# Local and global attention with a gated layer behind it: first loads through another queue, strips by copies, weights in eight loads

## The chip, the core and the metric

The kernel runs on one core of a Trainium2 chip. The time is the device time of one execution in microseconds; less is better. The core has five engines with queues of their own: TensorE (PE), VectorE (DVE), ScalarE (ACT), GpSimd (POOL) and SyncE (SP). PEld in the profile is TensorE's weight load. Transfers are issued here by SyncE and by GpSimd, and both queues share 16 DMA engines. A transfer that changes the type of the data (float32 to float16) is issued by GpSimd in this kernel; SyncE's keep the type.

## What is computed

```
# q_l, k_l, v_l: (8 batches, 8 heads, 512, 64); q_g, k_g, v_g: (8, 8, 32, 64); float32
k_all, v_all = concat(k_g, k_l), concat(v_g, v_l)
out_g = softmax(q_g k_all^T / 8) v_all                      # 32 global rows see everything
s_ll  = where(|i - j| <= 32, q_l k_l^T / 8, -1e9)           # 512 local rows: a band of 65 keys
out_l = softmax(concat(q_l k_g^T / 8, s_ll)) v_all          # and the 32 global keys
x = concat(out_g, out_l), heads side by side                # (8 * 544, 512)
h = x @ w_in                                                # (4352, 2048)
out = (h * clip(h + 3, 0, 6) / 6) @ w_out                   # (4352, 512)
```

## The kernel before

**Layout and stages.** Matmul operands are float16. A batch has four tiles of 128 local rows (`j`), and each tile four units of 32 rows (`u`). For each tile the steps are:

- load: `load_qk` (two transfers of 128 x 8 x 64 values, q into `nat[:, 0]` and k into `nat[:, 1]`), `load_v` into `ve`, `load_g` into `natg`;
- turn: `turn_qk` transposes eight 128 x 128 blocks on TensorE (L471) into the one PSUM tile `t` and copies them to `qk`; `turn_g` does the same for the global rows (L487, `gt`);
- scores: `local_step` writes into PSUM `s`. Where `kept` is true (`b < KEPT`) each unit's 96 keys stand in the order in which the strip holds them, cut in pieces, with 32-row matmuls for the global keys (L527, 80 matmuls a tile); otherwise 8 matmuls (L534) and 32 (L541);
- softmax, for each of eight heads: VectorE adds the mask, takes the minimum of the negated scores and writes `sm` (L553); ScalarE takes exponentials (L564); VectorE scales four heads at a time into `pn` (L578); TensorE transposes (L585); a copy takes `et` out of `t`;
- values: `av` multiplies `et` with strips `st`: for each unit, the 96 rows of v that it may see and the 32 global rows (L603 in batches 0 and 1, L608 later). The result goes from PSUM `a` to `xt`.

`global_steps` does the 32 global rows of a batch. The strips are made from `ve` in one of two ways: `strips_kept`, copies on ScalarE or VectorE, or `strips_moved`, seven transfers by SyncE's queue (L435).

The gated layer follows: `first` multiplies with `win` (L713), ScalarE computes `t` (L720), VectorE the product `gs` (L724); `second` multiplies `gs` with `wout` (L735), a copy takes `ot` out and SyncE stores it (L750). Batch 0 goes through `first` in parts of 128 rows, batch 1 of 256, the others of 512 (`PART`).

**Order.** Nothing is scheduled on the chip. Each step is added to a `Plan` with the engines that can do it, a duration for each (ns), its predecessors, a key (lower is more urgent) and the rings of buffers that it takes and frees. `Plan.lay` goes through time and writes the order of each engine's instructions; a step that two engines can do (`BOTH`) goes to one of them by a rule. `Transfers` stands in for the DMA queues, eight in flight on each. `Plan.fill` puts matmuls on a tile of zeros (`idle`, L850) into gaps of TensorE that the plan shows before the first step of the gated layer. On the chip each engine runs its list in that order and waits where a predecessor isn't done: a constant changed in the plan moves instructions everywhere.

**Beginning.** GpSimd's queue starts with q and k of tile 0, then the selects that make `ident` and the mask's band, then k_g, tile 1 and the rest by `seq` (`v` a part of v, `i` a quarter of w_in, `g` the other global rows). VectorE clears tiles (`clear`) and makes six masks (`mask_steps`): 3 to 5 for the kept order, 0 to 2 for the other. w_in comes in 16 transfers of 128 x 512 values (`load_w_in`), w_out in 16 (`load_w_out`), w_out behind batch 1's loads by its keys.

Of the kernel before, what the change touches and what calls it, by code (L numbers as in the profile page):

```python
# [26 lines left out]
class Transfers:  # L27
# [4 lines left out]
    FIRST, SHARE = {"POOL": 2400, "SP": 2700}, {"POOL": 0.65, "SP": 0.35}  # L32
# [41 lines left out]
class Plan:  # L74
# [4 lines left out]
    COLD, FILL = 5150.0, 216.0  # L79
# [17 lines left out]
    def lay(self):  # L97
        free = {e: 1240 if e == "POOL" else 0 for e in self.LAT}
# [27 lines left out]
        while len(order) < len(self.ops):  # L126
            best = None
            behind = {e: sum(o.can[e] for o in cand if len(o.can) == 1 and not o.dma) for e, cand in opened.items()}
            for e, cand in opened.items():
# [5 lines left out]
                for o in cand:  # L135
                    s = max(free[e], ready[o])
                    if len(o.can) > 1 and any(max(free[k], ready[o]) + d + behind[k] < s + o.can[e] + behind[e]
                                              for k, d in o.can.items() if k != e):
                        continue
                    if o.acq:  # L140
                        s = max(s, min(rings[o.acq]))
                    if o.dma:
                        t = move.lane_free(o, e)
                        s = INF if t is None else max(s, t)
                    if s < INF:
                        starts.append((s, o))
# [3 lines left out]
                s, o = min(((s, o) for s, o in starts if s <= s0 + 40), key=lambda x: (x[1].key, x[1].n))  # L150
                if best is None or s < best[0]:
                    best = (s, o, e)
# [20 lines left out]
            else:  # L173
                o.fin = s + dur + self.LAT[o.eng]
# [4 lines left out]
    def fill(self, order, emit):  # L179

        at, out = 900.0, []
        for o in order:
            if o.eng == "PE" and at is not None:
                one = self.FILL * (2 if at < self.COLD else 1)
                for _ in range(int((o.start - at - 150) / one)):
                    out.append(Op("PE", one, emit, (), 0, None, (), 0, None))
                at = None if o.acq == "M" else max(at, o.start + o.dur)
# [5 lines left out]
def kernel(  # L193
# [83 lines left out]
    def copy(op, out, in_):  # L277
        if op.eng == "ACT":
            nc.scalar.copy(out=out, in_=in_)  # L279
        else:  # L280
            nc.vector.tensor_copy(out=out, in_=in_)  # L281

    BOTH = ("ACT", "DVE")
    SCALE = ("DVE", 600)
# [10 lines left out]
    def mask_steps():  # L295
# [5 lines left out]
        z = add("DVE", 250, a, key=-9)  # L301
# [7 lines left out]
        z = add("POOL", 700, b, [z], key=-7.98)  # L309
# [7 lines left out]
        z = add("DVE", 700, c, [z], key=-9)  # L317

        def d():
            nc.vector.tensor_copy(out=masks[5], in_=m)  # L320
            nc.vector.memset(masks[5][P - UQ:P, UQ:2 * UQ], OUTSIDE)
            for u in range(NU):
                nc.vector.tensor_copy(out=w[u * UQ:(u + 1) * UQ, G:P], in_=m[0:UQ, 0:KL])
            nc.vector.tensor_copy(out=masks[0], in_=w)
            nc.vector.memset(masks[0][0:UQ, G:G + UQ], OUTSIDE)
            nc.vector.tensor_copy(out=masks[2], in_=w)
            nc.vector.memset(masks[2][P - UQ:P, P - UQ:P], OUTSIDE)
        prep["masks"] = add("DVE", 1000, d, [z], key=-3.5)
        return z

    def ident_step():
# [7 lines left out]
        return add("POOL", 400, b, [z], key=-7.99)  # L339

    def clear():
        for r in range(2):
# [3 lines left out]
            nc.vector.memset(kgz[r], 0.0)  # L346
            nc.vector.memset(pg[r][:, S:], 0.0)
            nc.vector.memset(ve[r][:, NJ, :], 0.0)
        nc.vector.memset(natg[0], 0.0)

    prep["ident"] = ident_step()
    prep["clear"] = add("DVE", 2000, clear, key=-10)
# [8 lines left out]
    ROW, WIDE, LONG, STORE, SHORT = 13.6, 80.0, 175.0, 92.0, 72.0  # L361
# [23 lines left out]

    def load_v(b, i, key):
# [12 lines left out]
    TIGHT, AHEAD, KEPT, PART = 2, 6.0, 1, {0: 128, 1: 256}  # L399

    def strips_kept(b, js, key):
# [8 lines left out]
        def put(dst, src, deps):  # L410
            o.append(add(BOTH, (160 + 730 * n, 60 + 140 * n), lambda op: copy(op, dst, src), deps + before,
# [41 lines left out]
    def load_w_in(g, key):  # L453
        return [load(lambda op, m=m: w_in_t[:, m, g * 512:(g + 1) * 512],
                     moe_w_in[m * P:(m + 1) * P, g * 512:(g + 1) * 512], P, key + 0.001 * m, ns=WIDE)
                for m in range(NP)]

    def load_w_out(c, key):
        return load(lambda op: w_out_t[:, c, :], moe_w_out[c * P:(c + 1) * P, :], P, key, ns=WIDE)
# [3 lines left out]
    def turn_qk(b, j, ld, key):  # L463
        r = b % 2

        def pe(op):
            ps = psT[op.slot]
            for i in range(2):
                for p in range(NP):
                    c0 = (i * NP + p) * P  # L470
                    nc.tensor.matmul(out=ps[:, c0:c0 + P], lhsT=nat[ld[0].slot][:, i, p * P:(p + 1) * P],  # L471
                                     rhs=ident, is_transpose=True)
        t = add("PE", 450, pe, [*ld, prep["ident"]], key=key, acq="T", rel=ld[:1])

        def ev(op):
            copy(op, qk[r][:, :, :, UQ + j * P:UQ + (j + 1) * P],
                 psT[t.slot].rearrange("d (i p s) -> d p i s", i=2, p=NP))
# [3 lines left out]
        return add(BOTH, (900, 600), ev, deps, key=key, rel=[t])  # L481
# [28 lines left out]
    def local_step(b, j, key):  # L510
# [3 lines left out]
        m_op = prep["mask"] if kept and j < NJ - 1 else prep["masks"]  # L514
# [29 lines left out]
        s = add("PE", 900 if kept else 600, pe, [qkT[b, j], qkT[b, min(j + 1, NJ - 1)], kg[b]], key=key, acq="S")  # L544
# [4 lines left out]
        for h in range(H):  # L549
# [10 lines left out]
            t = add("DVE", 212, red, [s, sm_op, m_op], key=key + 0.01 * h, rel=[s])  # L560
# [70 lines left out]
    def global_steps(b, key):  # L631
# [5 lines left out]
        for e in range(2):  # L637
# [10 lines left out]
            s = add("PE", 360, pe, [gT[b // 2]] + [qkT[b, j] for j in range(NJ)], key=key + 0.2 * e, acq="S")  # L648
# [81 lines left out]
    def second(t0, gdone, set_, dests, keys):  # L730
        f = None
        for q in range(4):
# [4 lines left out]
            deps = gdone[q * 4:q * 4 + 4] + [wo[c] for c in range(q * 4, q * 4 + 4)]  # L737
# [50 lines left out]
    lqk, lg = {}, {}  # L788
# [98 lines left out]
```

## Time and profile before

| | before |
|---|---|
| median of 3 runs | 366.24 us (363.99 to 366.33) |
| profiled execution: time, span | 366.75 us, 365.0 us |
| granted clock of TensorE, mean | 0.984 |
| TensorE busy | 342.1 us (94%), 4407 matmuls |
| VectorE, ScalarE, GpSimd busy | 286.1, 249.9, 120.9 us |
| moved by DMA | 41.89 MB: 17.57 by GpSimd's queue, 23.60 by SyncE's |
| matmuls on the idle tile | 51, 14.4 us |

The span is the time from the first to the last instruction. Matmuls are pipelined and their ends are modelled, so a busy TensorE may also be one that waits. In lines of the profile, `out<-in` names tiles without buffer numbers, shapes are partitions x elements, `L` numbers are lines of the kernel, and the part in brackets is the idle time of the engine before the instruction and what ended it. Copies of the helper `copy` all have line L281 on VectorE and L279 on ScalarE, and every load by GpSimd has L365.

### The profile page before, as it was taken

The numbers are of one execution on the slowest core, as the hardware profiler recorded it, in microseconds if no ns is written. First come the engines' busy times: TensorE is split into PE (matmuls) and PEld (weight loads), VectorE is DVE, ScalarE is ACT, GpSimd is POOL, SyncE is SP. The second block draws the span as 40 slices with busy tenths as digits, with TensorE's granted clock in tenths as the row PEclk, the third lists the DMA queues.
The fourth block names the chain that finished last, engine by engine and source line by source line (L and its number), as shares of the span: only waits on it lengthen the run. The fifth ranks groups of instructions, "written<-read, shape, count | busy, mean of one in ns | idle before, by whom it ended". The sixth has DMA issues, their size and how long they took to land.

```text
span 365.0 us, 11304 instructions
## 1 busy us (share of the span) xinstructions
PE 342.1 (94%) x4407; PEld 204.1 (56%) x4407; DVE 286.1 (78%) x1018; ACT 249.9 (68%) x772; POOL 120.9 (33%) x167
## 2 busy tenths in 40 slices
PE   6985986999899999999999999999999999999995
PEld 2555883556885665456555654555455444445642
DVE  7799888679898999788898989889988996166300
ACT  0686885679895799687976797558974885165411
POOL 8978855870293603135421531060000000000000
PEclk9999897899999999999999999999999999999999
DMA  9999999999699999539991999099001100110012
GB/s 65 138 175 135 171 224 206 99 190 247 86 139 225 138 179 203 39 75 166 234 68 59 141 225 105 31 132 246 32 2 59 61 2 0 59 57 0 31 48 97
DMA packets 123205, 41.89 MB, mean 115 GB/s; under 512 B 108432, under 2 KB 116112, under 8 KB 123152
## 3 DMA queue, kind: packets, MB, share of 16 engines
q0 software_dynamic: 111104, 17.57, 65.6%
q1 hardware_dynamic: 12048, 23.60, 22.8%
q8 instruction: 34, 0.56, 0.6%
q14 instruction: 19, 0.16, 0.2%
HBM read 35.13 MB, written 8.91 MB: 121 GB/s over the span
## 4 chain that ended last, share of the span: by engine, by line
PE 60%; DVE 19%; DMA 6%; ACT 6%; POOL 4%; issue 3%; SPq 0%; POOLq 0%; ACTq 0%; DVEq 0%
PE m L735 28%; PE m L713 20%; DVE gs L724 5%; DVE sm L553 4%; DMA win<-in_moe_w_in_dram 3%; DVE pn L578 3%; PE t L585 3%; DVE xt L281 2%; ACT sm L564 2%; PE a L608 2%; POOL nat L365 2%; ACT t L720 2%; PE t L471 2%; DMA st<-ve 2%; PE s L541 1%
## 5 line engine op out<-in xcount | busy, mean ns | idle before, releaser
L735 PE MATMUL m<-wout,gs 128*128 128x512 f16 x544 | 131.7, 385 | 0.6 <-DVE gs L724 0.6
L713 PE MATMUL m<-xt,win 128*128 128x512 f16 (+2 forms) x768 | 124.9, 310 | 5.5 <-DVE gs L724 3.2
L564 ACT ACTIVATE sm<-sm,stat 128x128 f32<-128x128 f32 x256 | 99.8, 393 | 20.1 <-DVE stat L553 19.9
L724 DVE SCALAR_TENSOR_TENSOR gs<-t,m 128x512 f16<-128x512 f32 x136 | 90.7, 682 | 23.4 <-ACT t L720 22.7
L713 PEld LDWEIGHTS <-win 128*128 128x128 f16 x832 | 69.2, 99 | 51.8 <-issue 8.2
L720 ACT ACTIVATE t<-m 128x512 f32<-128x512 f32 x136 | 80.0, 595 | 23.9 <-PE m L713 21.2
L735 PEld LDWEIGHTS <-gs 128*128 128x128 f16 x544 | 50.4, 99 | 51.7 <-issue 2.9
L553 DVE CUSTOM_DVE_ANT_0 sm<-s,mask 128x128 f32<-128x128 f32 x256 | 60.0, 284 | 8.4 <-PE s L541 7.9
L365 POOL DMA_DIRECT2D nat<-in_q_l_dram x32 | 28.7, 898 | 102.0 <-PE t L471 95.3
L564 ACT ACTIVATION_READ_ACCUMULATOR sm<-sm,stat 128x1 f32 x256 | 48.7, 190 | 0.0
L578 DVE TENSOR_TENSOR pn<-sm,stat 128x512 f16<-128x512 f32 x64 | 44.0, 688 | 1.1
L365 POOL DMA_DIRECT2D ve<-in_v_l_dram x40 | 32.4, 835 | 0.1
L279 ACT CAST xt<-a 64x512 f16<-64x512 f32 (+1 forms) x36 | 20.8, 577 | 15.7 <-PE a L608 12.5
L279 ACT COPY ot<-m 128x512 f32<-128x512 f32 x21 | 12.2, 582 | 25.9 <-PE m L735 23.0
L365 POOL DMA_DIRECT2D nat<-in_k_l_dram x32 | 29.2, 911 | 0.1
L585 PE MATMUL t<-ident,pn 128*128 128x128 f16 x256 | 20.3, 222 | 3.5 <-issue 1.7
L585 PEld LDWEIGHTS <-pn 128*128 128x128 f16 x256 | 17.0, 99 | 9.6 <-issue 4.5
L471 PE MATMUL t<-ident,nat 128*128 128x128 f16 x256 | 19.9, 219 | 1.6 <-DMA nat<-in_k_l_dram 1.4
L553 DVE DVE_READ_ACCUMULATOR2_ANT stat<- 128x1 f32 x256 | 21.0, 82 | 0.0
L471 PEld LDWEIGHTS <-nat 128*128 128x128 f16 x256 | 16.3, 98 | 7.5 <-DMA nat<-in_k_l_dram 1.7
L281 DVE COPY et<-t 128x1024 f16<-128x1024 f16 x22 | 15.1, 687 | 6.7 <-PE t L585 5.7
L281 DVE CAST xt<-a 64x512 f16<-64x512 f32 (+1 forms) x20 | 13.8, 690 | 5.4 <-ACT xt L279 4.4
(76 smaller groups left out, 322.1 us busy)
## 6 DMA issues: line engine op xcount, KB each, us to landing
out_dram<-ot SPq DMA_DIRECT2D x32, 256.0 KB, 3.1
st<-ve SPq DMA_DIRECT2D x14, 384.0 KB, 6.4
nat<-in_q_l_dram POOLq DMA_DIRECT2D x32, 128.0 KB, 4.9
nat<-in_k_l_dram POOLq DMA_DIRECT2D x32, 128.0 KB, 5.1
st<-ve SPq DMA_DIRECT2D x7, 512.0 KB, 6.8
st<-ve SPq DMA_DIRECT2D x14, 256.0 KB, 6.1
ve<-in_v_l_dram POOLq DMA_DIRECT2D x24, 128.0 KB, 4.9
win<-in_moe_w_in_dram POOLq DMA_DIRECT2D x16, 128.0 KB, 5.3
```

The lines of the kernel that those rows point to most:

```text
L279: nc.scalar.copy(out=out, in_=in_)
L281: nc.vector.tensor_copy(out=out, in_=in_)
L365: nc.gpsimd.dma_start(out=dst(op), in_=src)
L471: nc.tensor.matmul(out=ps[:, c0:c0 + P], lhsT=nat[ld[0].slot][:, i, p * P:(p + 1) * P], rhs=ident, is_transpose=True)
L553: nc.vector.tensor_tensor_reduce(out=sm[sm_op.slot][:, h, :], in0=psS[s.slot][:, e, p * P:(p + 1) * P], in1=m, scale=-scale, scalar=3.0e38 ...
L564: nc.scalar.activation(out=sm[sm_op.slot][:, h, :], in_=sm[sm_op.slot][:, h, :], func=EXP, scale=-1.0, bias=stat[stat_op.slot][:, 0, h:h + 1],
L578: (nc.gpsimd if op.eng == "POOL" else nc.vector).tensor_tensor(out=pn[pn_op.slot][:, h0:h1, :], in0=sm[sm_op.slot][:, h0:h1, :], in1=stat[ ...
L585: nc.tensor.matmul(out=psT[op.slot][:, h * P:(h + 1) * P], lhsT=pn[pn_op.slot][:, h, :], rhs=ident, is_transpose=True)
L713: nc.tensor.matmul(out=psM[op.slot][:, i * n:(i + 1) * n], lhsT=w_in_t[:, m, (c + i) * P:(c + i + 1) * P], rhs=x()[:, m, t0:t0 + n], start ...
L720: nc.scalar.activation(out=t1[to.slot], in_=psM[f.slot], func=RELU, bias=0.5, scale=1.0 / 6.0)
L724: nc.vector.scalar_tensor_tensor(out=gs[set_.slot][:, c:c + k, t0:t0 + n], in0=t1[to.slot].rearrange("f (k t) -> f k t", k=k), scalar=1.0, ...
L735: nc.tensor.matmul(out=psM[(f or op).slot], lhsT=gs[set_.slot][:, c, t0:t0 + P], rhs=w_out_t[:, c, :], start=(c == 0), stop=(c == NDFF - 1))
```

## The change

1. **q and k of tiles 0 and 1 of batch 0** are loaded by SyncE's queue as float32 into `sm` (free at that time), and VectorE or ScalarE casts them into `nat` (`load_qk_direct`). `turn_qk` can turn q or k alone: of tile 1, k is loaded and turned ahead of q, and the scores of tile 0 wait for the k parts of both tiles (`keyT`) and their own q part.
2. **Strips of batch 1** are copied too (`KEPT` from 1 to 2, so that batch 1's scores take the kept form), in blocks of one, one and two tiles instead of two and two. GpSimd may do these copies as well (`COPY`).
3. **Masks and clears.** Only masks 3 and 4 are made at the start; the others follow behind the first scores, in pieces that ScalarE or VectorE does (`later`). Some clears become ScalarE copies from `idle`. The selects stand ahead of GpSimd's first load.
4. **Weights** come in four transfers for w_in and four for w_out, 512 rows of 512 values each.
5. **Filled gaps.** The filling goes on until tile 0 of batch 2 is multiplied with its strips, for gaps over 400 ns, and the idle matmuls write `a` instead of `m`.
6. **The plan** has other durations and shares for DMA, and a step that two or three engines can do goes to the one that would end it first, counting only more urgent work ahead of it.

By the order of the instructions, GpSimd has 17 of the strip copies (5 for batch 0, 12 for batch 1). In the whole kernel VectorE has 10 more copies into `et`, 6 more into `eg`, 4 more into `ot` and 7 more of 64 rows into `xt`, and 7 fewer of 1024 columns into `qk`. TensorE has 56 idle matmuls.

```diff
@@ class Transfers, class Plan
-    FIRST, SHARE = {"POOL": 2400, "SP": 2700}, {"POOL": 0.65, "SP": 0.35}
+    FIRST, SHARE = {"POOL": 2400, "SP": 2400}, {"POOL": 0.55, "SP": 0.45}
-    COLD, FILL = 5150.0, 216.0
+    COLD, FILL = 5000.0, 216.0
+    AHEAD, WAIT = 0.3, 0.0
@@ lay
-                    if len(o.can) > 1 and any(max(free[k], ready[o]) + d + behind[k] < s + o.can[e] + behind[e]
-                                              for k, d in o.can.items() if k != e):
-                        continue
+                    if len(o.can) > 1:
+                        ends = {k: max(free[k], ready[o]) + d + sum(
+                            x.can[k] for x in opened[k] if len(x.can) == 1 and not x.dma and x.key < o.key
+                            and ready[x] < max(free[k], ready[o]) + 100) for k, d in o.can.items()}
+                        if min(ends.values()) < ends[e]:
+                            continue
@@ fill
-                for _ in range(int((o.start - at - 150) / one)):
-                    out.append(Op("PE", one, emit, (), 0, None, (), 0, None))
-                at = None if o.acq == "M" else max(at, o.start + o.dur)
+                if o.start - at > 400:
+                    out += [Op("PE", one, emit, (), 0, None, (), 0, None) for _ in range(int((o.start - at - 200) / one))]
+                at = None if o is until else max(at, o.start + o.dur)
@@ mask_steps
+        def later(after):
+            def full(k, src, rows_, cols, key, deps):
+                z = add(BOTH, (300, 250), lambda op: copy(op, masks[k], src), deps, key=key)
+                return add("DVE", 85, lambda: nc.vector.memset(masks[k][rows_, cols], OUTSIDE), [z], key=key)
...
@@ new
+    def load_qk_direct(b, j, key):
+        ld, o = [], {}
+        for n, i in enumerate((0, 1) if j == 0 else (1, 0)):
+            def emit(op, i=i):
+                nc.sync.dma_start(out=rows(sm[(ld[0] if ld[0] is not op else op).slot].rearrange("s h d -> s (h d)")[
+                    :, i * HD:(i + 1) * HD]), in_=heads((q_l, k_l)[i][b, :, j * P:(j + 1) * P, :]))
+            ld.append(add("SP", 600, emit, (), key=key + 0.001 * n, acq=None if n else "sm", dma=(P * H, ROW)))
+            if n == 0:
+                na = add("DVE", 0, lambda op: None, ld[:1], key=-7, acq="nat")
+
+            def ev(op, i=i):
+                copy(op, nat[na.slot][:, i, :], sm[ld[0].slot].rearrange("s h d -> s (h d)")[:, i * HD:(i + 1) * HD])
+            o[i] = add(BOTH, (580, 360), ev, [ld[n], na], key=-7, rel=ld[:1])
+        return [na, o[0], o[1]]
@@ strips
-    TIGHT, AHEAD, KEPT, PART = 2, 6.0, 1, {0: 128, 1: 256}
+    TIGHT, AHEAD, KEPT, PART, W_OUT = 2, 6.0, 2, {0: 128, 1: 256}, -6.0
+    BLOCKS = ((0,), (1,), (2, 3))
-            o.append(add(BOTH, (160 + 730 * n, 60 + 140 * n), lambda op: copy(op, dst, src), deps + before,
+            o.append(add(COPY, (150 + 450 * n, 90 + 165 * n, 150 + 550 * n)[:len(COPY)], lambda op: copy(op, dst, src),
+                         deps + before,
@@ weights
-        return [load(lambda op, m=m: w_in_t[:, m, g * 512:(g + 1) * 512],
-                     moe_w_in[m * P:(m + 1) * P, g * 512:(g + 1) * 512], P, key + 0.001 * m, ns=WIDE)
-                for m in range(NP)]
+        return [load(lambda op: w_in_t[:, :, g * 512:(g + 1) * 512],
+                     moe_w_in[:, g * 512:(g + 1) * 512].rearrange("(m k) f -> k m f", k=P), NP * P, key, ns=WIDE)]
-    def load_w_out(c, key):
-        return load(lambda op: w_out_t[:, c, :], moe_w_out[c * P:(c + 1) * P, :], P, key, ns=WIDE)
+    def load_w_out(g, key):
+        return load(lambda op: w_out_t[:, g * 4:(g + 1) * 4, :],
+                    moe_w_out[g * 512:(g + 1) * 512, :].rearrange("(c f) d -> f c d", f=P), 4 * P, key, ns=WIDE)
@@ the batches
-            seq = ["q0", "k", "q1", "v0", "v1", "q2", "v2", "q3", "v3", "v4", "i0", "i1", "i2", "i3", "g"]
+            seq = ["q0", "q1", "k", "v0", "v1", "q2", "v2", "q3", "v3", "v4", "i0", "i1", "i2", "i3", "g"]
-                    lqk[0, i] = load_qk(0, i, key)
+                    lqk[0, i] = (load_qk_direct if i < 2 else load_qk)(0, i, key)
+            if b == 0 and j < 2:
+                na, lq, lk = lqk[0, j]
+                keyT[0, j] = turn_qk(0, j, [na, lk], lead - 1.5 + 0.1 * j, (1,))
+                qkT[0, j] = turn_qk(0, j, [na, lq], lead + j - 1.4, (0,))
...
-    order = plan.fill(plan.lay(), lambda: nc.tensor.matmul(out=psM[2], lhsT=idle[:, 0:P], rhs=idle))
+    order = plan.fill(plan.lay(), lambda: nc.tensor.matmul(out=psA[0][:, 1, :], lhsT=idle[:, 0:P], rhs=idle),
+                      av_last[TIGHT, 0])
```

## The prediction

> **What bounds the kernel now.** I read the page, then engine times by stretch, then the first 100 us instruction by instruction. The page:
>
> ```profile
> span 365.0 us, 11304 instructions
> PE 342.1 (94%) x4407; PEld 204.1 (56%) x4407; DVE 286.1 (78%) x1018; ACT 249.9 (68%) x772; POOL 120.9 (33%) x167
> ```
>
> By stretch (length, then busy us and instruction count of each engine, granted clock, DMA share, GB/s):
>
> ```profile
> 40.00:50.00 10.00, 10.00 (x230) 9.42 (x228) 9.04 (x28) 8.50 (x18) 6.25 (x12) 1.00 1.46 193
> 50.00:60.00 10.00, 5.75 (x134) 5.16 (x132) 7.11 (x32) 7.89 (x33) 4.54 (x8) 0.98 1.15 229
> 60.00:70.00 10.00, 9.72 (x134) 5.04 (x140) 7.27 (x31) 3.99 (x20) 7.33 (x10) 0.68 1.40 121
> 90.00:100.00 10.00, 8.70 (x201) 7.80 (x199) 8.19 (x29) 8.09 (x19) 2.28 (x3) 1.00 0.72 121
> 100.00:300.00 200.00, 196.55 (x2406) 112.75 (x2405) 177.87 (x629) 156.04 (x507) 54.99 (x70) 1.00 0.86 117
> ```
>
> From 100 us on TensorE is busy 98% of the time: there it sets the pace, and whatever is won earlier is kept to the end. What can be won lies before 100 us, where it idles, runs idle matmuls (51 of them, 14.4 us in the groups by line), or only looks busy. The largest such place (TensorE's, SyncE's and GpSimd's timelines; start, length):
>
> ```profile
> 61.04 5.30 PE L735 MATMUL m<-wout,gs 128*128 128x512 f16 x12
> ...
> 47.99 8.95 SPq L435 DMA_DIRECT2D st<-ve  x6
> ...
> 48.26 0.53 POOL L365 DMA_DIRECT2D wout<-in_moe_w_out_dram  x1 [2.17 <-DMA ve<-in_v_l_dram]
> ```
>
> Twelve matmuls that take 2.6 us elsewhere in the chain (its piece of 12 at 190.44) take 5.30, with no other engine named: the chunks of wout land one by one. While GpSimd issues them, SyncE issues batch 1's strips, and a wout chunk takes up to 13.1 us from issue to landing:
>
> ```profile
> DMA to landing us min/median/max: 5.7/7.8/13.1
> ```
>
> Ahead of it VectorE paces the attention of batch 0. Its timeline, and its groups by shape in the first 60 us (busy, mean ns):
>
> ```profile
> 11.35 0.69 DVE L281 COPY qk<-t 128x1024 f16<-128x1024 f16 x1 [1.53 <-PE t L471]
> 12.05 2.36 DVE L281 COPY st<-ve 96x1024 f16<-96x1024 f16 x4
> ...
> L578 DVE TENSOR_TENSOR pn<-sm,stat 128x512 f16<-128x512 f32 x10 | 6.8, 683 | 0.1
> L281 DVE COPY st<-ve 32x1024 f16<-32x1024 f16 x11 | 5.4, 489 | 0.2
> ```
>
> The first scores start at 11.88 and end at 12.77, but VectorE's first masked minimum starts at 14.34: four strip copies stand between. A later wait for strips:
>
> ```profile
> 92.27 0.54 PE L608 MATMUL a<-et,st 128*128 128x64 f16 x13 [1.28 <-DMA st<-ve]
> ```
>
> **The change, part by part**, by the order in which the new program's instructions stand on each engine and the durations above.
>
> *Loads.* Tiles 0 and 1 of q and k leave GpSimd's queue: four issues of 0.9 us. The two q/k loads and the select of ident, which stood ahead of k_g, become three selects (0.32, 0.29, 0.26 us) first in the queue; k_g's issue moves from 4.02 to about 2.3, and the first w_in issue from 14.72 to about 11.3. Weights: 16 issues of w_in at 0.58 become 4. Loads with 1024 packets issue in 0.9 us, with 128 in 0.55, so one with 512 lies between; I take 0.7. DMA then limits: batch 1's q and k, issued back to back, land 0.83 to 0.85 us apart, w_in chunks 0.65. Batch 0 (about 12 loads) needs 10.5 us, w_in 10.4, batch 1 11, wout 10.4, the small ones 1.5: from about 3 us everything is there by 47, plus the last latency 48. GpSimd's five copies in batch 0's strips now stand among batch 1's loads. The trace has no copy on GpSimd: at VectorE's speed one costs 0.4 us, by the slope of the two selects (0.27 us at 96 columns, 0.32 at 128) 1.7. I take 1.2, nearer the selects as the same engine's rows. So wout is there between 46 and 53 instead of 65.3 (the last landing), before it is wanted (below). That cover is 4 us; without it each us late is a us lost.
>
> *First scores.* SyncE's 256 KB stores land after 3.1 us, GpSimd's first load 3.6 after its issue: q0 between 4.0 and 4.6, k0 0.85 later. New: a cast from single precision (no row; 0.4 to 0.7 us, between a strip copy and a PSUM cast; I take 0.5), then q0, k_g, k0, k1 through the one PSUM tile t: 4 x (0.4 transpose + 0.42 copy + 0.4 hand-offs) = 4.9. Scores start near 10.0 against 11.88. Only one short strip copy is left behind them: the first masked minimum at 11.3 against 14.34.
>
> *Attention of batch 0.* From there to the last scaling of tile 3 VectorE's stream holds 32 minima at 0.21 (6.7), 8 scalings at 0.69 (5.5), reciprocals 1.2, three copies out to et (2.1), q/k copies 2.5, nine strip copies 3.2, masks 1.1, the rest 3.3: 25.6 us, so 36.9; tile 3's transposes start at 41.78 now. ScalarE's stream (32 exponentials at 0.39, 4.1 of strip and mask copies, 3.0 of others) is done by 31. Clears and masks that went to ScalarE lie in its 12 us of idle at the start.
>
> *To the second layer.* From tile 3 to the first L735 the new order has on VectorE 11 gs (7.5), 16 minima (3.4), and 7.2 of copies, scalings and global steps: 18. ScalarE from 26.5: 16 t at 0.595 (9.5), 23 exponentials (8.9), nine strip copies of batch 1 (5.0), others 4.5: 27.9, so 54.4. TensorE: 208 matmuls of 128 columns at 0.056 (11.7), three kept score steps at 0.88, and 5: 19.4. All three end between 54 and 56; I add 2 for waits among them and for idle matmuls. These now write psA and so wait for its copy-out, and eight new ones stand on the way, 0.22 us each. L735 starts near 57.0 and finds its weights. Now it is as if it had started unhindered at 66.34 - 2.6 = 63.7. **Gain 6.7** (3 to 9.5).
>
> *Smaller terms.* Tile 0 of batch 1 is through its 32 L603 before this point, not after: -0.7. Batch 2's strips then have SyncE's queue and DMA for themselves: -1.3, the wait at 92. Batch 1's fourth kept score step: 80 matmuls in 0.88 against 40 in 0.63: +0.25. The new rule for the shared copies gives VectorE 10 more et (6.9 us), 6 eg (2.9), 4 ot (2.7) and 7 xt (4.8), and 7 fewer qk (-4.8), over all batches, and ScalarE less. Cover: VectorE's 22 us of idle in the 200 from 100 to 300. It takes 1.6 us per batch out of 4; I charge 1.0 in all (0 to 12, see the rivals). Nothing for the clock: it is 1.00 from 70 on but in the tail, and the dip at 60 to 70 goes with the stall already counted.
>
> Sum against the profiled execution's 366.75 (span 365.0, 1.75 around it, 0.5 above the median of the runs): -6.7 - 0.7 - 1.3 + 0.25 + 1.0 = **359.3**; I say 359.
>
> **Rivals.**
>
> *More.* The engines' waits of 2 us don't come and VectorE's new copies cost nothing: L735 at 54.5. 366.75 - 9.2 - 0.7 - 1.3 + 0.25 = 355.8. For it: 40 to 50 has TensorE busy 10.00 of 10. Against: 50 to 60, and one t tile for every transpose.
>
> *GpSimd's copies hold up VectorE.* VectorE's timeline has one mask copy twice, beside a GpSimd issue and free of it:
>
> ```profile
> 4.94 0.61 DVE L315 COPY mask<-mask 128x128 f32<-128x128 f32 x1
> ...
> 5.63 0.19 DVE L320 COPY mask<-mask 128x128 f32<-128x128 f32 x1
> ```
>
> 0.42 us more. Seventeen GpSimd copies, five before 26 us and twelve from 37 to 53, each stopping one VectorE instruction that long: 7.1 us on the engine that paces this stretch; 359.3 + 7.1 = 366.4, no change. Against: the scalings hardly vary (667 to 694 ns) beside GpSimd's issues. [...]
>
> *The weights still come late.* GpSimd's copies cost 2 us or more each and batch 1's loads and wout slip past their cover by 4 us: 363.3. Against: the cover above, and fewer issues.
>
> *Slower: VectorE becomes the bound from batch 1 on.* 85 gs in 100 to 300 are 5.3 batches, 37.6 us each, of which VectorE is busy 33.5. With 1.6 more it has 35.1; if its 4.1 of waits (for scores, t and xt) don't shrink, a batch takes 39.2. 7.5 batches x 1.6 = 12: 358.3 + 12 = 370.3. It decides where these waits stay above 2.5 us per batch. Against: an et copy takes 0.69 on VectorE, 1.01 on ScalarE, and shortens the chain that causes such waits.
>
> **How the numbers follow.** The forecast 0.54, more 0.20, held-up VectorE 0.11, late weights 0.05, VectorE as bound 0.10. Faster by over 1% (below 362.6; about what a measurement can tell) are the first two, 0.74; within 1% the next two, 0.16; slower 0.10. The range goes from 352.5 (gain 9.5 and a VectorE that costs nothing give 355.5; 3 more for the bounds of casts and loads) to 368, above the two middle rivals.
>
> **What would show it.** First L527 near 10, first minimum of L592 near 11.3, tile 3's L624 near 37; the first twelve L774 in under 3.5 us, starting 55 to 59; last wout landing before 53; no wait for st near 90; TensorE at least 97% busy from 100 us on. Wrong if L774 starts after 61, if GpSimd's copies exceed 2 us, or if VectorE's waits from 100 us on make TensorE fall under 95%.

## The result, and the profile after

The changed kernel takes 367.81 us (median of 20 runs, 365.52 to 372.37), the kernel before 366.01 us beside it (20 runs, 363.42 to 369.04). The ratio is 1.0049, with a 95% interval of 1.0025 to 1.0073: slightly slower, where 359 had been forecast. Runs more than 1.5% above the fastest of their kernel stand in the medians but not in the ratios (one of the changed kernel's 20, and four of the 12 of e5 below, whose profile is one of the four and is not used). The profiled executions took 366.60 us, against 366.75 before: this pair of traces does not show the 1.8 us by which the medians differ. The page of the changed kernel begins (compare the same two lines in the prediction):

```profile
span 364.8 us, 11632 instructions
PE 345.3 (95%) x4572; PEld 204.7 (56%) x4572; DVE 301.0 (83%) x1042; ACT 248.5 (68%) x775; POOL 119.2 (33%) x156
```

VectorE is busy 15 us more, and TensorE has 165 matmuls more: 160 of them are the kept form of batch 1's four score steps (40 each), five are idle matmuls. The stretches, as before:

```profile
40.00:50.00 10.00, 9.95 (x251) 8.36 (x250) 9.88 (x36) 8.07 (x20) 4.80 (x7) 1.00 1.39 186
50.00:60.00 10.00, 9.04 (x242) 8.39 (x239) 9.56 (x32) 9.08 (x28) 9.54 (x15) 1.00 0.66 43
60.00:70.00 10.00, 9.90 (x226) 6.73 (x224) 9.95 (x35) 9.88 (x32) 10.00 (x13) 1.00 1.83 141
90.00:100.00 10.00, 10.00 (x203) 8.97 (x201) 9.86 (x38) 9.20 (x29) 3.16 (x5) 1.00 0.47 52
100.00:300.00 200.00, 195.14 (x2372) 109.34 (x2370) 181.84 (x635) 146.72 (x482) 50.60 (x64) 1.00 0.83 115
```

The hole at 50 to 60 and the half clock at 60 to 70 are gone, as forecast. But VectorE (the third engine) is now 96 to 99% busy in the four stretches shown up to 100, and from 100 to 300 TensorE is busy 1.4 us less than before. TensorE's timeline where the first expert block meets its weights:

```profile
42.29 0.61 PE L624 MATMUL t<-ident,pn 128*128 128x128 f16 x8
...
62.02 1.04 PE L774 MATMUL m<-wout,gs 128*128 128x512 f16 x4
...
63.29 1.03 PE L774 MATMUL m<-wout,gs 128*128 128x512 f16 x4
...
64.78 1.46 PE L774 MATMUL m<-wout,gs 128*128 128x512 f16 x6
```

L774 runs unhindered, as said (its starts lie 0.22 us apart), but begins at 62.02, not 57.0. To say where time goes I use an estimate: TensorE's loss in a stretch is the stretch less the time of its useful matmuls, each taken at the median spacing of starts of its shape in these two traces (0.216 us for 512 columns, 0.056 for 128). By 100 us it has lost 41.5 us before and 37.8 after: the start brings 3.7 us, not 8.45 (6.7 + 0.7 + 1.3 - 0.25). From 100 to 300 it loses 16.9 before and 19.3 after, and most of the gain is gone.

### The profile page after: what moved, and what is told of

It reads as the page before. It is cut to its first block, busy times and chain, and to the rows that moved or that the text cites. A ratio compares the mean times of both kernels' runs of the same rounds, so it can differ in the third digit from the quotient of the medians.

```text
span 364.8 us, 11632 instructions
## 1 busy us (share of the span) xinstructions
PE 345.3 (95%) x4572; PEld 204.7 (56%) x4572; DVE 301.0 (83%) x1042; ACT 248.5 (68%) x775; POOL 119.2 (33%) x156
## 4 chain that ended last, share of the span: by engine, by line
PE 44%; DVE 36%; ACT 12%; issue 3%; DMA 2%; POOL 1%; SPq 0%; POOLq 0%; ACTq 0%
PE m L752 17%; PE m L774 17%; DVE gs L763 8%; DVE sm L592 7%; ACT sm L603 7%; DVE pn L617 7%; DVE xt L289 4%; DVE st L289 3%; DVE et L289 2%; PE t L624 2%; ACT xt L285 2%; DVE ot L289 2%; PE t L508 2%; DMA ve<-in_v_l_dram 2%; PE a L647 1%
## 5 line engine op out<-in xcount | busy, mean ns | idle before, releaser
L774 PE MATMUL m<-wout,gs 128*128 128x512 f16 x544 | 130.2, 379 | 0.4
L763 DVE SCALAR_TENSOR_TENSOR gs<-t,m 128x512 f16<-128x512 f32 x136 | 91.2, 682 | 22.8 <-ACT t L759 22.1
L774 PEld LDWEIGHTS <-gs 128*128 128x128 f16 x544 | 49.4, 98 | 50.3 <-DVE gs L763 1.8
L383 POOL DMA_DIRECT2D nat<-in_q_l_dram x30 | 26.7, 890 | 106.3 <-PE t L508 103.2
L617 DVE TENSOR_TENSOR pn<-sm,stat 128x512 f16<-128x512 f32 x64 | 46.7, 730 | 0.9
L383 POOL DMA_DIRECT2D nat<-in_k_l_dram x30 | 27.0, 899 | 0.0
L285 ACT COPY ot<-m 128x512 f32<-128x512 f32 x17 | 9.9, 582 | 22.6 <-PE m L774 19.3
L289 DVE CAST xt<-a 64x512 f16<-64x512 f32 (+1 forms) x26 | 18.0, 693 | 5.7 <-ACT xt L285 5.0
L285 ACT CAST xt<-a 64x512 f16<-64x512 f32 (+1 forms) x30 | 17.2, 572 | 7.5 <-DVE xt L289 4.3
L289 DVE COPY et<-t 128x1024 f16<-128x1024 f16 x32 | 21.9, 685 | 0.3 <-PE t L624 0.2
L894 PE MATMUL a<-idle 128*128 128x512 f16 x56 | 18.7, 477 | 2.0 <-DVE idle L352 1.2
```

The source lines that it names most:

```text
L383: nc.gpsimd.dma_start(out=dst(op), in_=src)
L617: (nc.gpsimd if op.eng == "POOL" else nc.vector).tensor_tensor(out=pn[pn_op.slot][:, h0:h1, :], in0=sm[sm_op.slot][:, h0:h1, :], in1=stat[ ...
L763: nc.vector.scalar_tensor_tensor(out=gs[set_.slot][:, c:c + k, t0:t0 + n], in0=t1[to.slot].rearrange("f (k t) -> f k t", k=k), scalar=1.0, ...
L774: nc.tensor.matmul(out=psM[(f or op).slot], lhsT=gs[set_.slot][:, c, t0:t0 + P], rhs=w_out_t[:, c, :], start=(c == 0), stop=(c == NDFF - 1))
```

## The experiments

Ratios are to the kernel before on the same chip, with 95% intervals. Differences between experiments are between medians from different chips, where the kernel before had medians of 365.81 to 366.57; e4, e9, e10, e12, e15 and e16 have four runs each. By the widths of the intervals such a difference is good to 1 to 3 us. Theory P: GpSimd's copies stop VectorE. Theory V: VectorE's time, which the new test for shared copies spends, is what runs short. Others came up on the way.

### GpSimd's copies

VectorE's and GpSimd's timelines of the changed kernel:

```profile
17.74 3.06 DVE L617 TENSOR_TENSOR pn<-sm,stat 128x512 f16<-128x512 f32 x1
```

```profile
16.67 1.70 POOL L287 COPY st<-ve 32x512 f16<-32x512 f16 x2
18.32 0.88 POOL L383 DMA_DIRECT2D nat<-in_k_l_dram  x1
19.19 2.50 POOL L287 COPY st<-ve 128x1024 f16<-128x1024 f16 x2
```

A scaling that takes 0.68 elsewhere takes 3.06 beside them; tile 0's transposes start at 24.53 against 19.09, after a wait for a VectorE copy that stands behind it. Five kernels ask what that is worth.

```diff
         elif op.eng == "POOL":
-            nc.gpsimd.tensor_copy(out=out, in_=in_)
+            nc.vector.tensor_copy(out=out, in_=in_)    # e1; e3: nc.gpsimd.memset(out, 0.0)
+            # e4: the tensor_copy twice; e5: nc.sync.dma_start(out=out, in_=in_)
-    COPY = ("ACT", "DVE", "POOL")
+    COPY = BOTH                                        # e2 alone, planned anew
```

> The plan and every engine's order stay as changed; the 17 strip copies that GpSimd had are issued at the same places on VectorE (0.25 to 0.49 us each, 6 us in all). Theory 1 (GpSimd's copies stop VectorE while they run: 5 us of longer VectorE instructions between 9 and 25 us): no scaling (L617) over 0.8 us, tile 3's transposes near 39 instead of 42.3, first L774 near 59 instead of 62.0, time 3 us below the changed kernel, about 364.5. Theory 2 (VectorE's larger share of the work is what costs; GpSimd's copies relieve it): VectorE has 6 us more to do, so first L774 at 62 or later and time 367 to 371.

> COPY names ScalarE and VectorE alone, and the plan is laid anew. Theory 1: as with the copies moved by hand, 3 to 4 us below the changed kernel, about 364. Theory 2: no gain, 367 to 370.

> GpSimd writes zeros where it copied, in the same places (so these parts of the strips are zero): it writes SBUF but reads nothing. Theory 1 in the form that a GpSimd instruction that reads SBUF stops a VectorE instruction with two SBUF inputs: the scaling of 3.06 us is back at 0.69, time 2 to 3 us below the changed kernel (365). Theory 1 in the form that any GpSimd instruction does it: the scaling stays over 2 us as far as the zeros take as long, time as changed (367.5). Theory 2: as changed.

> Each of GpSimd's 17 copies is issued twice in a row. Theory 1: VectorE's long instructions between 15 and 25 us grow by another 3 to 5 us, time 370 to 373. Theory 2: VectorE's work is the same; GpSimd is 13 us busier in a queue with 15 us of idle before 60 us, so 367.5 to 369.

> Same plan and order; the 17 strip copies that GpSimd had are transfers on SyncE's queue, so neither GpSimd nor VectorE does them. Theory 1 (only the stops by GpSimd's copies cost) failed in e1, where they went and 6 us of copies came to VectorE instead. Theory 3 (VectorE's time before 100 us is what counts: 94 of 100 us busy in the changed kernel against 84 before, whether stops, copies or the shifted shared copies fill it): VectorE has 5 to 6 us less before 60 us than in the changed kernel and in e1, first L774 near 59, time 3 to 4 us below the changed kernel, 363.5 to 364.5. Rival, theory 4 (the order in which TensorE's list stands, first L752 and idle matmuls ahead of tile 2's transposes, holds the attention of batch 0 whatever VectorE does): first L774 stays at 62 to 64 as in e1, time 367 to 368.

| kernel | us | ratio |
|---|---|---|
| e1, on VectorE | 367.66 | 1.0032 [1.0008, 1.0055] |
| e2, planned without GpSimd | 369.97 | 1.0101 [1.0058, 1.0143] |
| e3, zeros | 366.48 | 1.0025 [0.9987, 1.0063] |
| e4, twice | 373.90 | 1.0215 [1.0157, 1.0273] |
| e5, by SyncE | 370.12 | 1.0050 [1.0007, 1.0094] |

In e3 parts of the strips are zeros, so its outputs are other numbers. The groups by shape of the first 60 us, busy and mean ns, of the changed kernel, then of e3, then of e1:

```profile
L617 DVE TENSOR_TENSOR pn<-sm,stat 128x512 f16<-128x512 f32 x10 | 9.6, 957 | 0.1
```

```profile
L617 DVE TENSOR_TENSOR pn<-sm,stat 128x512 f16<-128x512 f32 x10 | 6.8, 685 | 0.1
L289 DVE COPY st<-ve 32x512 f16<-32x512 f16 x6 | 4.6, 764 | 0.0
```

```profile
L289 DVE COPY st<-ve 32x512 f16<-32x512 f16 x6 | 1.7, 285 | 0.0
```

With zeros in place of GpSimd's copies the scalings are back at 685 ns (683 in e1, 957 beside the copies). But the zeros slowed VectorE's own strip copies, 764 ns against 285 where GpSimd does nothing to the strips (566 beside its copies). So theory P is right about the stops: 2.7 us over the ten scalings. Taking them away (e1, e5) gains nothing: in e1 tile 0's transposes start at 20.57, four us earlier, and L774 at 64.03, later than the 62.02 of the changed kernel. e1 puts the copies on VectorE, but e5 does not. So P does not explain the missing gain. Doubling the copies (e4) costs 6 us, but not by longer stops of scalings, which take 804 ns there on average. TensorE waits for a load that GpSimd issues later, and half rate comes with it (68.7 to 75.6, a mean granted clock of 0.91 from 60 to 100; the trace is of the slowest of four runs):

```profile
PE t L525 <- DMA natg<-in_k_g_dram: 3.8, 1, 3.8
```

e8 asks it the other way: the kernel before, with GpSimd allowed among batch 0's strip copies.

```diff
-            o.append(add(BOTH, (160 + 730 * n, 60 + 140 * n), ...
+            o.append(add(("ACT", "DVE", "POOL"), (160 + 730 * n, 60 + 140 * n, 150 + 550 * n), ...
```

> The kernel before, in which GpSimd too may take the strip copies of batch 0 (the plan is laid anew). Theory 1: stops of VectorE's scalings and copies of 1 to 3 us each beside the GpSimd copies, 2 to 4 us slower than before. Theory 3: GpSimd takes work from VectorE, which was busy 84 of the first 100 us, and stops it about as long: within 1 us of before. In both, scalings (L578) over 1 us stand beside the GpSimd copies.

366.77 us, 1.0018 [0.998, 1.0057]: no difference. It tells little, since the plan gave GpSimd one copy only, and no scaling beside it grew (0.67 to 0.69 us):

```profile
L281 POOL COPY st<-ve 32x1024 f16<-32x1024 f16 x1 | 1.1, 1117 | 0.0
```

### The test for shared copies

Of the 32 copies into `et`, VectorE did 22 before. By tile, in the changed kernel, and with only the old test put back (e6):

```profile
L289 DVE COPY et<-t x32: 672/684/692, 25.7 to 302.9; 128x1024 f16<-128x1024 f16 x32
```

```profile
L287 DVE COPY et<-t x23: 672/683/692, 23.1 to 280.7; 128x1024 f16<-128x1024 f16 x23
L283 ACT COPY et<-t x9: 992/1007/1060, 103.4 to 298.2; 128x1024 f16<-128x1024 f16 x9
```

```diff
-                    if len(o.can) > 1:
-                        ends = {k: max(free[k], ready[o]) + d + sum(...
...
+                    if len(o.can) > 1 and any(max(free[k], ready[o]) + d + behind[k] < s + o.can[e] + behind[e]
+                                              for k, d in o.can.items() if k != e):
+                        continue                       # e6; e7: and the copies of GpSimd by SyncE as in e5
```

> Only the rule by which the plan gives a shared step to an engine is the old one (it counts all waiting work of an engine, not only the more urgent); the plan is laid anew, 23 instead of 32 et copies on VectorE, 14 GpSimd copies. Theory 3: VectorE is relieved by some 8 us over the kernel, most of it after 60 us; it is idle again for several us between 60 and 100, time 1 to 3 us below the changed kernel, 365 to 366.5. Theory 4: no change or worse, 367 to 369, as tile 2 of batch 0 still comes late.

> e5 and e6 together. Theory 3: 4 to 6 us below the changed kernel, 362 to 364, faster than before. Theory 4: 366 to 369.

e6: 363.64 us, 0.9921 [0.9891, 0.995]. e7: 361.76 us, 0.9873 [0.9823, 0.9922]. The old test alone is worth 4.2 us (367.81 - 363.64). With it, SyncE's queue for GpSimd's copies brings another 1.9 us (e7, six runs; the intervals overlap). e9 is the kernel before with the new test and nothing else; e10 the changed kernel in its own order, with et copies moved by hand. The edit takes twelve of them, in batches 2 to 7, not the eight of the last two batches that the expectation names:

```diff
+            if b >= 2 and j % 2 == 0:                  # e10
+                nc.scalar.copy(out=et[...], in_=psT[t.slot])
...
```

> The kernel before with one thing changed: the test in the planner by which a copy that two engines may do is given to VectorE or ScalarE is the changed kernel's. There are no copies on GpSimd. Theory V (VectorE's time is what the changed kernel ran short of, and the new test spends it): more of the et copies stand on VectorE than the 22 of 32 of before, VectorE is busier between 100 and 300 us by 3 us or more than its 177.9, TensorE loses 2 to 5 us more there, time 368.5 to 371.5. Theory P (the changed kernel lost only by GpSimd's copies stopping VectorE): nothing to lose here, 366 to 367.5.

> The changed kernel in its own order, with every second et copy of the last two batches (8 of 32) issued on ScalarE at the same place of the order instead of VectorE; the copies of GpSimd stay. Theory V: 8 x 0.68 = 5.4 us leave VectorE between 100 and 300 us, TensorE's loss there falls from 9.2 us by 2 to 4, time 363.5 to 366. Theory P: the first 100 us are the same instructions, so the time stays at 367 to 368.5; slower (369 to 371) if the ScalarE copies of 1.0 us delay the exponentials behind them instead.

e9: 370.13 us, 1.0140 [1.0069, 1.0212]. The new test alone costs some 5 us, without any GpSimd copy. TensorE's waits from 100 to 300 (total, times, longest), of e9 and then e6; before has 2.4 in 5, the changed kernel 2.9 in 7:

```profile
PE m L715 <- DVE gs L726: 4.8, 8, 1.0
```

```profile
PE m L750 <- DVE gs L761: 1.3, 3, 0.8
```

And the stretch from 100 to 300, e9 and then e6:

```profile
100.00:300.00 200.00, 193.26 (x2435) 111.44 (x2433) 177.37 (x642) 149.45 (x492) 53.77 (x68) 1.00 0.84 116
```

```profile
100.00:300.00 200.00, 197.72 (x2414) 112.69 (x2411) 176.87 (x630) 160.56 (x506) 53.93 (x68) 1.00 0.84 116
```

The time is as theory V said, the way is not. VectorE is no busier there in e9 (177.4 against 177.9 before), but the experts' products gs reach TensorE later. By the estimate above TensorE loses more from 100 to 300 wherever the new test stands: 3.5 us in e9 against before, 3.9 in the changed kernel against e6, 4.7 in e14 against e12 (both in the next section). That is where the test costs. The traces of e9 and e10 are of the slowest of their four runs, so these sizes are rough.

e10: 371.45 us, 1.0159 [1.0086, 1.0232]. VectorE's busy time from 100 to 300 fell from 181.8 to 172.9 us, and TensorE lost 3.4 us more there than in the changed kernel, at full clock. But the copies take longer on ScalarE, and TensorE now waits for them too:

```profile
L631 ACT COPY et<-t x12: 990/998/1017, 79.2 to 298.4; 128x1024 f16<-128x1024 f16 x12
PE a L650 <- ACT et L631: 0.7, 4, 0.2
```

So e10 shows that ScalarE can't take these copies in this order; it does not refute V, since it slows ScalarE's chain as well, as its expectation allowed for. Whether the test costs by VectorE's time (in the changed kernel 181.8 us against 176.9 in e6) or by its order, and why gs comes later, is not settled.

### Strips of batch 1

```diff
-    TIGHT, AHEAD, KEPT, PART, W_OUT = 2, 6.0, 2, {0: 128, 1: 256}, -6.0
+    TIGHT, AHEAD, KEPT, PART, W_OUT = 2, 6.0, 1, {0: 128, 1: 256}, -6.0   # e12 with the old test, e14 without
```

> The changed kernel with the old test for shared copies and with the second batch's strips brought by transfers, as before, so that only the first batch's are copied. Theory V: some 8 strip copies leave VectorE, ScalarE and GpSimd between 60 and 100 us, VectorE's busy time there falls by 2 to 4 us, time 361 to 363 against 363.6. Rival (the strips' transfers come late, as where before waited near 92 us): 364 to 366.

> The changed kernel with one thing undone: the second batch's strips come by transfers as before; the new test for shared copies stays. If the test and the strips cost separately (4.1 and 4.8 us): 362 to 364. If the test costs only where VectorE is already full of strip copies: 358.5 to 360.5. If the test costs as much without them as it did in the kernel before (5 us): 363.5 to 365.

e12: 358.84 us, 0.9804 [0.9729, 0.9879]. e14: 364.87 us, 0.9958 [0.9933, 0.9984]. Undoing the copied strips is worth 2.9 us with the new test and 4.8 with the old, so each edit costs by itself. e16 is e12 with no copies on GpSimd; e11 is e6, and e15 is e12, with the old rule for idle matmuls, which then write `m` again and end at the first expert block.

```diff
-                if o.start - at > 400:
-                    out += [Op("PE", one, emit, ...) for _ in range(int((o.start - at - 200) / one))]
-                at = None if o is until else max(at, o.start + o.dur)
+                for _ in range(int((o.start - at - 150) / one)):
+                    out.append(Op("PE", one, emit, (), 0, None, (), 0, None))
+                at = None if o.acq == "M" else max(at, o.start + o.dur)     # e11, e15, e17, e18
```

> Old test, the second batch's strips by transfers (358.8 us), and no copies on GpSimd at all: the first batch's strip copies are shared by VectorE and ScalarE, planned anew. Theory P (GpSimd's copies stop VectorE): seven copies less beside VectorE, 357 to 358.5. Theory V (VectorE's time in the first 40 us is what counts): seven copies more on VectorE and ScalarE, some 4 us of their time, 359.5 to 361.5.

> The changed kernel with the old test for shared copies (363.6 us alone) and also the old rule for the idle matmuls, which end at the first expert block's first matmul as before. Theory T (the order on TensorE and its idle matmuls in the first 60 us cost some of the start's gain): first L774-like matmul of the experts earlier by 1 to 2 us, time 361.5 to 363. Rival: the idle matmuls only fill gaps, and without them the granted clock comes up later; 363.5 to 366.

> Old test, the second batch's strips by transfers (358.8 us), and the old idle matmuls, which end at the first expert block. Where this was done with copied strips it gave 362.7 instead of 363.6 us. Theory T (idle matmuls stand ahead of work that is ready): 357 to 358.5. Rival, nothing left to gain because the first tiles wait for strips and not for TensorE: 358.5 to 360.

e16: 359.22 us, 0.9785 [0.9729, 0.9842], no different from e12. e11: 362.66 us, 0.9907 [0.987, 0.9945], and **e15: 356.31 us, 0.9686 [0.964, 0.9733]**, the fastest here. Its first L772 (the after's L774) starts at 56.78.

Is it the strips' copies that cost, or the kept form of the score steps? e13 (on e12) and e18 (on e15) take the form without the copies. The strips then lie in another order than the form takes, so batch 1's outputs are other numbers and only the time is read:

```diff
-        kept = b < KEPT
+        kept = b < 2
```

> As the kernel with the old test and the second batch's strips brought by transfers (358.8 us), but the second batch's score steps keep the changed kernel's form (eight heads' pieces and the global keys placed column by column, more matmuls each) although its strips now lie the other way; the outputs of that batch are therefore other numbers, and the run tells only the time. Theory V (the strips' copies cost the 4.8 us, by the time they take on VectorE, ScalarE and GpSimd): 358.5 to 360. Theory F (the form of the four score steps costs it): 361.5 to 364.

> Old test, old idle matmuls, second batch's strips by transfers (356.3 us), but its four score steps in the changed kernel's form, so that the outputs of that batch are other numbers and only the time is read. With the newer idle rule the form cost 7.9 us, in a profile that had 5.1 us more lost at half clock. Theory F1 (the form costs by its matmuls alone, 4 x 0.25 us, and the rest was the clock): 357 to 358.5 with the clock full. Theory F2 (80 matmuls in a row use up TensorE's instructions faster than they come, pauses of 2 to 3.5 us without a releaser follow, and the half clock follows them): such pauses again near 50 to 57 us, half clock after them, 360 to 364.

e13: 366.72 us, 0.9983 [0.9947, 1.0018]. e18: 365.80 us, 0.9983 [0.9942, 1.0023]. The form, with the plan laid anew for it, costs 7.9 and 9.5 us by the medians (6.6 and 10.9 by the ratios). With the copies beside it (e6, 363.64) it costs 3 us less than without (366.72). That is no wait for strips removed: TensorE waits for none in e13's trace from 25 to 100, and the pauses told below are 2.7 us in e6 against 5.9. The steps themselves take about what the prediction took, 0.84 against 0.65 us. Much of the rest is in TensorE's pauses. Its timeline in e18, and the instruction queue in the stretch from 47.6 to 48.7 (packets, MB, share):

```profile
45.46 0.40 PE L750 MATMUL m<-xt,win 128*128 128x128 f16 x4
50.02 0.29 PE L750 MATMUL m<-xt,win 128*128 128x128 f16 x1 [4.17 <-issue]
```

```profile
q8 instruction: 1, 0.02, 5.5%
```

Four matmuls into a block of 16, TensorE stops for 4.17 us, for nothing that the profile names ("issue"). One 16 KB packet of the instruction queue runs from 47.66 to 48.64, and TensorE goes on 1.38 us later. The other pauses look the same. Every one over 0.9 us without a releaser, between 25 and 100 us, in the kernel before, the changed one, e12, e13, e15, e16 and e18 ends 1.27 to 1.63 us behind such a packet (14 pauses of 0.9 to 4.2 us).

Their places tell more. I counted TensorE's records (matmuls, weight loads and those of its sequencer) in order of time. The 4.17 us stand behind record 1730, and other pauses behind 1986, 2242, 2754 and 3010, always a multiple of 256 apart to within one. In all 20 traces the 46 pauses of over 0.25 us without a releaser (from 14 us on) have 193 or 194 records before them, beyond a multiple of 256. And the queue's packets grow with TensorE's instructions, 34 for 8814 matmuls and weight loads before, 36 for 9144 after:

```profile
q8 instruction: 34, 0.56, 0.6%
```

```profile
q8 instruction: 36, 0.59, 0.7%
```

That is one packet for 259 and 254 of them. I read the pauses as TensorE waiting for its own next instructions, an estimate from these counts, since the profile names no releaser there. The form has 40 matmuls and 40 weight loads more in each of four steps, and with it these pauses grow from 3.8 us (e12) to 5.9 (e13), and from 3.0 (e15) to 10.0 (e18, whose profile is the slowest of its ten runs). Matmuls spaced out by the half rate (next section) cost 3.2 and 4.4 us more, and from 100 to 300 TensorE loses 2.7 and 3.2 us more, which neither explains. In the changed kernel itself the pauses are small: 1.0 us, against 0.3 in e14 and 3.1 before. So they explain what the form costs in e13 and e18, in part, and not what the strips cost there.

### The granted clock

Behind some of these pauses, and behind other idle time earlier, the traces have half rate (a granted clock of 0.50). The stretch from 25 to 60 us (granted clock third from the end) of e12, then e13, then e15:

```profile
25.00:60.00 35.00, 29.85 (x677) 25.27 (x676) 29.89 (x116) 28.08 (x90) 19.29 (x25) 0.93 1.51 178
```

```profile
25.00:60.00 35.00, 27.62 (x657) 23.72 (x655) 27.29 (x110) 23.91 (x73) 19.77 (x26) 0.84 1.52 179
```

```profile
25.00:60.00 35.00, 29.83 (x682) 25.19 (x680) 32.43 (x132) 30.04 (x99) 19.70 (x26) 1.00 1.51 178
```

The clock's records show half rate from 22.8 to 29.6 in e12; from 11.0 to 14.4, 24.7 to 31.5 and 55.4 to 62.2 in e13, the last out of a pause of 3.5 us (53.3 to 56.9); none in e15 until the tail. That fits e15's 2.5 us below e12. So do single runs: of e12's four, the one with a mean clock of 0.999 took 355.24 us, the others (0.986 to 0.990) 358.47 to 359.52, and e16's took 357.60 and 358.23 at 0.995 and 0.999, 360.21 and 361.41 at 0.988 and 0.981. Pauses of TensorE and half rate come together in these traces, so this does not price the clock by itself. e17 undoes the rule for idle matmuls alone.

> The changed kernel with one thing undone: the idle matmuls follow the old rule (every gap of the plan over 150 ns, up to the first expert block, and into the experts' PSUM tile). Theory C (the granted clock: in the changed kernel TensorE ran at half rate from 13.5 to 16.9 and from 23.7 to 30.6 us, which costs up to 1.7 and 3.4 us): the second stretch goes, the time falls by 1.5 to 3.5 us to 364.3 to 366.3; where the profile still shows half rate for as long, the time stays. Rival (VectorE sets the pace there, whatever the clock): 367 to 368.5 with the clock full.

e17: 368.67 us, 1.0059 [1.002, 1.0098]. No gain, but its profile still has half rate from 23.2 to 30.0, so the run tells that this rule alone does not bring the clock back, not what the clock would be worth.

The clock also sends us back to the kernel before, whose pause at 57.27 to 58.97 ended 1.43 us behind a packet that landed at 57.54. TensorE's timeline, then the stretches around it:

```profile
58.97 0.33 PE L585 MATMUL t<-ident,pn 128*128 128x128 f16 x3 [1.70 <-issue]
```

```profile
56.00:60.00 4.00, 1.60 (x24) 1.36 (x24) 2.63 (x17) 3.27 (x15) 0.85 (x1) 0.95 1.19 211
60.00:66.00 6.00, 5.72 (x52) 2.38 (x52) 4.20 (x18) 2.15 (x11) 3.57 (x6) 0.50 1.65 158
66.00:72.00 6.00, 6.00 (x138) 4.09 (x137) 5.04 (x24) 3.32 (x12) 5.75 (x8) 0.97 1.36 89
```

The twelve L735 that took 5.30 us start 0.427 us apart, all alike, and the following ones 0.216. That is half rate (59.6 to 66.4), not weights landing one by one: the last six landings lie 0.3 to 2.7 us apart, and, in the order of their issue, the twelfth chunk had landed at 60.15, before the first of the twelve matmuls started.

## Why the prediction was wrong, step by step

- **"Attention of batch 0"** is the step of the start that failed. VectorE's stream from the first minimum to tile 3's last scaling was sized at 25.6 us and took 28.9 (12.57 to 41.50). It was almost unbroken, as the sum assumed, but two of its terms were too small: eight scalings took 7.9 us (forecast 5.5), nine strip copies 5.0 (3.2). And it began late: the first scores start at 9.25 (10.0), but four fifths of the step wait until 11.01 for a copy into qk, and the first minimum comes at 12.57 (11.3; 14.34 before). So tile 3's transposes start at 42.29 (36.9) and L774 at 62.02 (57.0). The stretch between took 19.7 us, forecast 20.1. Against the 63.7 that the prediction takes for the kernel before, 1.7 us are left of the gain of 6.7. The stops by GpSimd are only a part: without its copies (e1) tile 3 comes at 40.91, with the old test (e6) at 37.74.
- **VectorE's share, +1.0** (0 to 12) is the second step that failed, by its size: the new test costs 4.2 us (e6), 6.0 beside moved strips (e14 less e12), some 5 on the kernel before (e9). Of the rivals only "VectorE becomes the bound" forecast a slower kernel. Its 12 us were too many, and its mechanism, a fuller VectorE, is not what e9 shows; in the changed kernel it is open.
- **Strips of batch 1, -1.3 and +0.25** have the wrong sum: they cost 2.9 to 4.8 us net. The wait at 92 did go, but e12 and e13 have no wait of more than 0.1 us for strips either, with transfers, so the copies weren't needed for it. The step's own duration was right. The form around it costs 7.9 and 9.5 us in e13 and e18, in part by TensorE's pauses without a releaser (5.9 and 10.0 us in all), which were in no rival.
- **"The chunks of wout land one by one"** was misread. The 5.30 us were half rate, behind a pause of 1.70 us without a releaser. The w_out loads did come early as forecast (last landing 50.9, forecast 46 to 53), but there was little to win by that.
- **"Nothing for the clock ... the dip at 60 to 70 goes with the stall"** failed. It went, and came back earlier: half rate at 13.5 to 16.9 and 23.7 to 30.6 in the changed kernel, 35.7 to 39.1 and 59.6 to 66.4 before, 10.2 us each without the tail. Tile 0's and 1's transposes took 1.0 us there against 0.6 for tiles 2 and 3.
- **GpSimd's copies**: 0.61 to 0.88 us for 512 columns and 1.03 to 1.21 for 1024 (means), below or at the 1.2 taken. The rival that they hold up VectorE came nearest in time, 366.4, by luck. The stops that it feared came: 10 scalings at 957 ns against 683 (e1) are 2.7 us. Its 0.42 us a stop does not follow from the two mask copies of 0.61 and 0.19, since the short one (5.63 to 5.82) lies beside a GpSimd issue too (5.50 to 6.38). As a cause of the end time it fell with e1.
- **What was right**: with the new test and the copied strips undone, the rest of the change gives 358.84 us (e12), and with the old idle matmuls 356.31 and L772 at 56.78, where the forecast had 359 and 57.0. The agreement is partly luck, since the stall that it was drawn from was another, and e15's last w_out load landed at 59.43, not by 53. Of the signs of being wrong only one came: L774 after 61. TensorE stayed 97.6% busy from 100 to 300, and still lost 2.4 us there; that sign was too coarse.

The traces of the changed kernel and of e14 differ by 1.5 us in span where the medians differ by 2.9, so one profile does not show all of what the strips cost there. That part, and why the new test's order delays gs, stay open.

## What to carry to other kernels

Look at the starts of a slow row of matmuls before naming its cause: here an even spacing of 0.427 us against 0.216 went with a granted clock of 0.50, while data landed 0.3 to 2.7 us apart. Then look at what idled TensorE just before. Where a pause has no releaser, count the engine's instructions up to it. Count a step's instructions as well as its duration: the form's 40 more matmuls a step add 0.2 us to it, and the two kernels with it took 7.9 and 9.5 us more. And a rule of a planner is part of the change like any kernel edit: price it by a run of its own, since here it cost 4 to 6 us of a change whose other parts can gain 10.

## What the runs showed of the hardware

- In seven traces (the kernel before, the changed one, e12, e13, e15, e16, e18) TensorE paused 14 times for 0.9 to 4.2 us without a releaser, and went on 1.27 to 1.63 us after a 16 KB packet of the instruction queue had landed. All 46 such pauses of over 0.25 us in the 20 traces stand a multiple of 256 of its records apart, to within one.
- The granted clock was 0.50 for 3.41 and for 6.83 us in the trace of before (35.7 to 39.1, 59.6 to 66.4), and as long in that of the changed kernel (13.5 to 16.9, 23.7 to 30.6), besides the end of each.
- Beside GpSimd's copies one scaling of VectorE took 3.06 us instead of 0.68; with GpSimd's memsets in their place the ten scalings took 685 ns on average (e3). VectorE's 32x512 strip copies took 285 ns without either (e1), 566 beside GpSimd's copies and 764 beside its memsets.
